# A tanh of a zero ahead of ScalarE's loads, and a first weight load in two pieces, in a decode attention and MLP kernel

## The chip, the cores and the metric

The kernel runs on one core of one Trainium2 chip. The metric is the device time of one execution in microseconds; the figure for a kernel is the median of its runs. Beside the times there is a profile of one execution, with its own time and its span (from its first to its last recorded instruction).

## What is computed

One decode step for two sequences (B = 2, one token each, D = 1024). A gate mixes an attention block with a cache (32 heads, 16384 cached positions, head size 128) and an MLP block. In short:

```python
def reference(A_x, A_k_cache, A_v_cache, A_wq, A_wo, B_x, B_w1, B_w2, B_w3, B_w4, gate_w):
    x = A_x                                                   # [2, 1, 1024], bf16
    g = sigmoid((x * gate_w).sum(-1, keepdims=True))
    q = (x @ A_wq) split into 32 heads
    a = softmax(q . k_cache * 128 ** -0.5) . v_cache, heads joined, @ A_wo
    hs = shift(gelu(layernorm(x) @ w1)) @ w2      # S is 1: the shift leaves only zeros
    x1 = x + hs
    b = x1 + gelu(layernorm(x1) @ w3) @ w4
    return g * a + (1 - g) * b
```

The caches are 2 x 268 MB in bf16, wq and wo 8.4 MB each, w2 2.1 MB, w3 and w4 7.3 MB each. All of it is read once.

## The kernel before, in words

**A plan written out by hand.** `_Plan` (line 24) holds a list of operations for each engine. `pl.add` (line 44) appends a compute operation and `pl.dma` (line 53) a transfer, each with the events that it waits for; `emit` (line 78) writes the lists out, so that the order of the calls in `build_kernel` is the order on each engine. A DMA raises its semaphore by 16, and the event is the sum up to then: an event on a semaphore that two DMAs raise one after the other waits for both.

**The ring.** All large data passes through one SBUF tile, `ring` (line 167): 5 slots, each 128 partitions x 16384 bf16, which is 32 KB a partition. `queue_load` puts a load into a list, `pump` (line 300) issues from it on SP as long as the slots of the next load are free, and `release` (line 311) frees slots at the event of the last reader. A slot has a semaphore (`s_ring`, line 225); loads in several pieces took those of `s_tail` (line 230), which before were only the pieces of the second half of wo. The order of the list is fixed: the two halves of wq into slots 0 and 1, w2 into slot 2, the halves of w3 into 3 and 4, those of w4 into 0 and 1 (line 335), then for each of 32 pairs of heads a K load and a V load (8.4 MB and two slots each), and at the end wo. SP issues nothing else but half of the output, so its queue is the stream of all weights and caches. A weight load is made by `runs` (line 321): partition p gets a run of neighbouring rows of the matrix, for a half of wq 4 rows of 4096 bf16, 32 KB in one piece, of a matrix in which the partitions lie 64 KB apart.

**The start.** GpSimd builds constants with a chain of memsets and selects (`pconst`, lines 238 to 275), the last being `xrow` at line 275. VectorE reduces some of them (lines 277 to 282; the reduction at line 277 waits for `ev_rowm`, that at line 279 for the whole chain). ScalarE's list begins with DMAs: x, two rows of 2 KB (line 560), the gate's weights, one row of 2 KB (line 561), and four pieces of x for the last sum (line 563), which wait for GpSimd's `xrow`. PE transposes x and the gate's weights (line 583) when both are there, VectorE copies the result into `xT_bf` and `xT_f` (lines 587 and 588), and PE multiplies the halves of wq with it (line 604: 256 matmuls; the last of a half releases the half's slot). The gate (`st_gate`, line 392) is a tanh on ScalarE (line 399), its first activation. The MLP's matmuls follow (lines 466, 495 and 537), with another tanh at line 448.

**The loop.** For a pair of heads VectorE transposes K in place in 8 pieces (`do_T`, line 647), PE makes the scores (`do_S`, line 653), the softmax goes through VectorE, PE and ScalarE (lines 663 to 680, with the exponential at line 674), PE multiplies with V (`do_PV`, line 689), and the result is scaled (`do_out`, lines 698 to 703). K's two slots are released one by one at line 653, V's at line 689. The end (`do_aproj`, lines 707 to 726) multiplies with wo and adds the MLP's part; line 750 copies the sum out.

Of the kernel before, what the change touches and what calls it, by code (L numbers as in the profile page):

```python
# [6 lines left out]
ACT = mybir.ActivationFunctionType  # L7
# [3 lines left out]
F32 = mybir.dt.float32  # L11
# [109 lines left out]
def build_kernel(nc, A_x, A_k, A_v, A_wq, A_wo, B_w1, B_w2, B_w3, B_w4, gate_w, out, dbg=None):  # L121
# [4 lines left out]
    HD = H * Dh  # L126
    assert Sq == 1 and Dh == 128 and D % 128 == 0 and F % 128 == 0 and B == 2
    P = 128
# [17 lines left out]
    scale = float(Dh) ** -0.5  # L146
    eps = 1e-5
    NEG_BIG = -30000.0
    RQ = NBD // 2
# [6 lines left out]
    assert QO * RO == Dh and RO == 2 * RS  # L156
    wo_runs = [[(0, RS)], [(RS, RS // 2), (RS + RS // 2, RS // 4), (RO - RS // 4, RS // 8), (RO - RS // 8, 1), (RO - 1, 1)]]
    assert all(sum(n for _, n in runs) == RS for runs in wo_runs)
    NQ = 4
    DQ = D // NQ  # L160
# [3 lines left out]
    with ExitStack() as st:  # L164
        block = st.enter_context(nc.Block())
        sb = lambda name, shape, dt: st.enter_context(nc.sbuf_tensor(name, shape, dt))
        ring = sb("ring", [P, NRS, SLOT], BF16)
# [51 lines left out]
        gin = sb("gin", [P, 2], F32)  # L219
        gT = sb("gT", [P, 4], F32)  # L220
        th = sb("th", [P, 2], F32)
        banks = [st.enter_context(nc.psum_tensor(f"ps{i}", [P, 512], F32)) for i in range(8)]
        sem = lambda n: st.enter_context(nc.semaphore(n))
        esems = {e: sem("e_" + e) for e in ENGS}
        s_ring = [sem(f"dr{i}") for i in range(NRS)]
# [4 lines left out]
        s_tail = [sem(f"dtl{i}") for i in range(len(wo_runs[1]))]  # L230
        pl = _Plan(esems)
# [6 lines left out]
        def pconst(fn, waits=()):  # L238
            pprev[0] = pl.add("pool", fn, waits=tuple(waits) + (pprev[0],), sig=True)
            return pprev[0]  # L240
# [29 lines left out]
        for hp in range(HP):  # L270
# [3 lines left out]
        pconst(aff(m24[:, :, :], 0, [[-1, 2], [-32, NQ]], 1), (e0,))  # L274
        ev_xr0 = pconst(lambda e: e.memset(xrow[:, :], 0.0))
        ev_const = pprev[0]
        e0 = pl.add("dve", lambda e: e.tensor_reduce(rowv[:, :], rowm[:, :, :].rearrange("p a b -> p (a b)"), axis=AX.X, op=ALU.add),
                    waits=(ev_rowm,), sig=True)
        ev_m2 = pl.add("dve", lambda e: e.tensor_reduce(m2[:, :], m24[:, :, :], axis=AX.X, op=ALU.add), waits=(ev_const,), sig=True)
# [3 lines left out]
                        waits=(e0,), sig=True)  # L283
# [16 lines left out]
        def pump():  # L300
            while dma_q and all(i in slot_free for i in dma_q[0][2]):
                key, fns, slots = dma_q.pop(0)
                waits = sum((slot_free.pop(i) for i in slots), ())
                slot_of[key] = slots[0]
                slots_of[key] = slots
                for k, fn in enumerate(fns):
                    dsem = s_ring[slots[0]] if len(fns) == 1 else s_tail[k]
                    dma_done[key] = dma_done[key, k] = pl.dma("sp", (lambda e, fn=fn, idx=slots[0]: fn(e, idx)), dsem,
                                                              waits=waits if k == 0 else ())

        def release(key, ev, slots=None):
            for idx in slots or slots_of[key]:
                assert idx not in slot_free
                slot_free[idx] = tuple(ev) if isinstance(ev, (tuple, list)) else (ev,)
            pump()
# [2 lines left out]
            assert key in dma_done, f"load {key} not yet issued in program order (would deadlock)"  # L318
            return dma_done[key]

        def runs(Wt, width, r0, rn, base=0):
            def fn(e, idx):
                src = Wt.rearrange("(p r) n -> p (r n)", p=P)[:, r0 * width:(r0 + rn) * width]
                return e.dma_start(ring[:, idx, (r0 - base) * width:(r0 - base + rn) * width], src)  # L324
            return fn

        wloads = {}
        for hi in range(2):
            wloads[("wq", hi)] = [runs(A_wq, HD, hi * RQ, RQ, hi * RQ)]
            wloads[("w3", hi)] = [runs(B_w3, F, hi * RQ, RQ, hi * RQ)]  # L330
            wloads[("w4", hi)] = [runs(B_w4, D, hi * RF, RF, hi * RF)]
            wloads[("wo", hi)] = [runs(A_wo, D, r0, rn, hi * RS) for r0, rn in wo_runs[hi]]
# [211 lines left out]
        key = ("w2", 0)  # L544
        put([row_stage(key, list(range(NBD)), 0, NBD, lambda kc: shT_bf[:, kc, :], "const", last=True), hs_columns], key)
        put([st_x1, ln_a(x1T_f[:, :, :], "x1", st2_ps, "xn2"), ln_b(st2_ps, "xn2", None)])
        for hi in range(2):
            key = ("w3", hi)
# [3 lines left out]
        for hi in range(2):  # L552
            key = ("w4", hi)
# [3 lines left out]
        put([st_bg])  # L557

        ev_bg0 = pl.add("dve", lambda e: e.memset(bgrow[:, :], 0.0), sig=True)
        ev_x = pl.dma("act", lambda e: e.dma_start(xg_row[0:2, :], A_x[:, 0, :]), s_misc)  # L560
        ev_gw = pl.dma("act", lambda e: e.dma_start(xg_row[2:3, :], gate_w.rearrange("(o d) -> o d", o=1)), s_gw)
        for qd in range(NQ):
            ev_xr = pl.dma("act", lambda e, qd=qd: e.dma_start(xrow[32 * qd:32 * qd + 2, :], A_x[:, 0, qd * DQ:(qd + 1) * DQ]), s_xr,
                           waits=(ev_xr0,))
# [8 lines left out]
        for pi in range(2):  # L573
            queue_load(("wo", pi), wloads[("wo", pi)], ((4, 3)[pi],))
        pump()

        def xcols(row, b_n, nb):
# [4 lines left out]
        for nb in range(NBD):  # L582
            last = pl.add("pe", lambda e, nb=nb: e.transpose(tr_ps[:, nb * 4:nb * 4 + 3], xcols(xg_row, 3, nb), ident[0:3, 0:3]),
                          waits=(ev_x, ev_gw, ev_ident), sig=(nb == NBD - 1))
# [10 lines left out]
        for hi in range(2):  # L595
            key = ("wq", hi)
            ev_arr = arrived(key)
            wv = ring_w(slot_of[key], RQ, HD)
            for r in range(RQ):
                kc = hi * RQ + r  # L600
                for h in range(H):
                    lastmm = (h == H - 1)
                    def fn(e, h=h, r=r, kc=kc, wv=wv, first=first):
                        return e.matmul(q_ps[:, h, :], lhsT=wv[:, r, h * Dh:(h + 1) * Dh], rhs=xT_bf[:, kc, :],  # L604
                                        start=first, stop=(kc == NBD - 1), skip_group_check=True)
# [6 lines left out]
        for bp in range(NBP):  # L612
            evp = pl.add("pe", lambda e, bp=bp: e.matmul(q4_ps[:, bp, :], lhsT=PermQ[:, bp, :],
                                                        rhs=q_sb[:, :, :].rearrange("p h b -> p (h b)"), start=True, stop=True),
                         waits=(ev_q, ev_const, ev_r0), sig=(bp == NBP - 1))
# [135 lines left out]
        for b, eng in enumerate(("sp", "act")):  # L751
            ev_out = pl.dma(eng, lambda e, b=b: e.dma_start(out[b, 0, :].rearrange("(q n) -> q n", q=NQ), orow[b:PR:32, :]), s_out[b],
                            waits=(ev_fin,))
# [28 lines left out]
def bass_gated_mix__mha_block_cached__mixer_s_mlp__decode_kernel(  # L782
    nc: bass.Bass,
    A_x: bass.AP,
    A_k_cache: bass.AP,
    A_v_cache: bass.AP,
    A_wq: bass.AP,
    A_wo: bass.AP,
    B_x: bass.AP,
    B_w1: bass.AP,  # L790
    B_w2: bass.AP,
    B_w3: bass.AP,
    B_w4: bass.AP,
    gate_w: bass.AP,
    out: bass.AP,
):
    build_kernel(nc, A_x, A_k_cache, A_v_cache, A_wq, A_wo, B_w1, B_w2, B_w3, B_w4, gate_w, out)
# [28 lines left out]
```

## Time and profile before

| what | value |
| --- | --- |
| median of 3 runs | 1326.1 us (1325.9 to 1326.19) |
| the profiled execution | 1325.93 us |
| its span | 1324.1 us |
| busy: PE, VectorE, ScalarE, GpSimd | 785.1, 657.2, 45.7, 23.5 us |
| DMA traffic | 570.60 MB, 431 GB/s over the span |

In the profile DVE is VectorE, ACT is ScalarE, POOL is GpSimd, PEld the weight loads of PE. SPq and ACTq are the issues of DMAs on SP and ACT, which count as no busy time. A row of a timeline gives the start and the time from the first to the last of its instructions in us, engine, line, operation, output <- input, their count, and in brackets how long the engine had been idle before and what ended it. A row of the windows gives the stretch, its length, busy time and count for each engine (PE, PEld, DVE, ACT, POOL), the granted clock of PE, the share in which the 16 DMA engines were busy, and GB/s. A row of the waits gives the engine and line, what it waited for, us in total, times, and the longest. A row of one line's instructions gives their durations in ns (min/median/max) and their first and last start.

### The profile page before, as it was taken

The numbers are of one execution on the slowest core, as the hardware profiler recorded it, in microseconds if no ns is written. First come the engines' busy times: TensorE is split into PE (matmuls) and PEld (weight loads), VectorE is DVE, ScalarE is ACT, GpSimd is POOL, SyncE is SP. The second block draws the span as 40 slices with busy tenths as digits, with TensorE's granted clock in tenths as the row PEclk, the third lists the DMA queues.
The fourth block names the chain that finished last, engine by engine and source line by source line (L and its number), as shares of the span: only waits on it lengthen the run. The fifth ranks groups of instructions, "written<-read, shape, count | busy, mean of one in ns | idle before, by whom it ended". The sixth has DMA issues, their size and how long they took to land.

```text
span 1324.1 us, 12290 instructions
## 1 busy us (share of the span) xinstructions
PE 785.1 (59%) x5235; PEld 335.8 (25%) x5235; DVE 657.2 (50%) x523; ACT 45.7 (3%) x99; POOL 23.5 (2%) x110
## 2 busy tenths in 40 slices
PE   3645557656556765555676555566655456665646
PEld 2512223222222322222232222222222222222223
DVE  1054446655444665544466554446655444665543
ACT  0000000000000000000000000000000000000000
POOL 3000000000000000000000000000000000000000
PEclk9966787777678777767877776788787788878679
DMA  9999999999999999999999999999999999999998
GB/s 403 445 424 434 436 434 434 432 438 432 430 440 432 430 440 430 430 440 430 434 436 430 438 434 436 432 432 438 434 428 440 432 430 440 430 432 438 430 434 359
DMA packets 11138, 570.60 MB, mean 431 GB/s; under 512 B 1252, under 2 KB 1268, under 8 KB 1655
## 3 DMA queue, kind: packets, MB, share of 16 engines
q1 hardware_dynamic: 11096, 570.43, 99.7%
q8 instruction: 8, 0.13, 0.0%
q10 hardware_dynamic: 30, 0.01, 0.0%
q14 instruction: 4, 0.02, 0.0%
HBM read 570.44 MB, written 0.00 MB: 431 GB/s over the span
## 4 chain that ended last, share of the span: by engine, by line
DMA 70%; PE 23%; DVE 6%; issue 0%; SPq 0%
DMA ring<-in_A_k_cache_dram 65%; PE ps L653 23%; DVE ring L647 6%; DMA ring<-in_B_w_dram 3%; DMA ring<-in_A_wo_dram 2%; PE ps L466 1%; SPq L324 0%; DVE orow L750 0%; PE ps L726 0%
## 5 line engine op out<-in xcount | busy, mean ns | idle before, releaser
L653 PE MATMUL ps<-ring,Z 128*128 128x512 bf16 x2048 | 534.5, 420 | 389.1 <-DVE ring L647 388.5
L647 DVE STREAM_TRANSPOSE ring<-ring 128x2048 f32<-128x2048 f32 x256 | 565.2, 2275 | 278.6 <-DMA ring<-in_A_k_cache_dram 278.6
L653 PEld LDWEIGHTS ps<-ring,Z 128*128 128x128 bf16 x2048 | 204.4, 104 | 706.7 <-issue 473.5
L689 PE MATMUL ps<-ring,PT_sb 128*32 128x512 bf16 x2048 | 168.2, 501 | 4.1 <-DVE recip L680 3.7
L703 DVE SCALAR_TENSOR_TENSOR OT_sb<-ps,gT,recip 128x2 f32 x32 | 7.0, 220 | 203.4 <-PE ps L700 203.4
L689 PEld LDWEIGHTS ps<-ring,PT_sb 128*32 128x32 bf16 x2048 | 67.6, 122 | 90.8 <-issue 69.6
L674 ACT ACTIVATE P_sb<-ps,negm 128x512 bf16<-128x512 f32 x32 | 22.0, 687 | 1013.9 <-DVE negm L672 1013.9
L663 DVE TENSOR_REDUCE rA<-ps 128x1 f32<-128x512 f32 x32 | 22.1, 692 | 64.1 <-PE ps L653 64.1
L678 PE MATMUL ps<-rowsum,hsel 128*128 128x1 f32 x128 | 24.0, 291 | 37.9 <-ACT P_sb L674 37.9
L676 DVE STREAM_TRANSPOSE PT_sb<-P_sb 128x512 bf16<-128x512 bf16 x32 | 22.8, 711 | 27.0 <-ACT P_sb L674 27.0
L634 POOL TENSOR_TENSOR Z<-q_f,mask 128x8 bf16<-128x8 f32 x64 | 12.3, 227 | 1214.3 <-PE ps L653 1214.3
L678 PEld LDWEIGHTS ps<-rowsum,hsel 128*128 128x128 f32 x128 | 21.3, 236 | 40.7 <-ACT P_sb L674 40.7
L665 PE MATMUL ps<-ident,rmax_bf 128*1 128x128 bf16 x32 | 6.9, 217 | 33.1 <-DVE rmax_bf L664 33.1
L698 ACT ACTIVATE acc_sb<-ps 128x512 bf16<-128x512 f32 x32 | 19.1, 597 | 198.8 <-PE ps L689 198.8
L700 PE MATMUL ps<-dsel,acc_sb 128*128 128x2 bf16 x128 | 8.1, 167 | 22.5 <-ACT acc_sb L698 22.5
L466 PE MATMUL ps<-xn_bf,ring 128*128 128x2 bf16 x224 | 14.5, 202 | 2.9 <-DMA ring<-in_B_w_dram 2.9
L466 PEld LDWEIGHTS ps<-xn_bf,ring 128*128 128x128 bf16 x224 | 14.4, 172 | 3.0 <-DMA ring<-in_B_w_dram 3.0
L700 PEld LDWEIGHTS ps<-dsel,acc_sb 128*128 128x128 bf16 x128 | 5.3, 96 | 38.2 <-ACT acc_sb L698 38.2
L665 PEld LDWEIGHTS ps<-ident,rmax_bf 128*1 128x1 bf16 x32 | 2.5, 79 | 48.9 <-DVE rmax_bf L664 48.9
L604 PE MATMUL ps<-xT_bf,ring 128*128 128x2 bf16 x256 | 7.1, 165 | 11.7 <-DVE xT_f L588 7.4
L666 DVE TENSOR_REDUCE m_sb<-ps 1x2 bf16<-1x128 bf16 x32 | 8.9, 278 | 9.9 <-PE ps L665 9.9
L672 DVE TENSOR_SCALAR negm<-ps,cAB 128x1 f32<-128x1 f32 x32 | 8.9, 277 | 9.2 <-PE ps L669 9.2
(97 smaller groups left out, 85.8 us busy)
## 6 DMA issues: line engine op xcount, KB each, us to landing
ring<-in_B_w_dram SPq DMA_DIRECT2D x4, 3584.0 KB, 35.4
ring<-in_A_wq_dram SPq DMA_DIRECT2D x2, 4096.0 KB, 17.5
ring<-in_A_wo_dram SPq DMA_DIRECT2D x1, 4096.0 KB, 40.2
ring<-in_B_w_dram SPq DMA_DIRECT2D x1, 2048.0 KB, 27.1
ring<-in_A_wo_dram SPq DMA_DIRECT2D x1, 2048.0 KB, 22.2
ring<-in_A_wo_dram SPq DMA_DIRECT2D x1, 1024.0 KB, 24.4
ring<-in_A_k_cache_dram SPq DMA_DIRECT2D x32, 26.8
ring<-in_A_v_cache_dram SPq DMA_DIRECT2D x32, 29.2
```

The costliest lines, as they stand in the source:

```text
L466: fn = lambda e, nb=nb, kl=kl: e.matmul(out_ps[:, nb, :], lhsT=cols(wv, kl, nb, nout), rhs=rhs_of(k0 + kl), start=False, stop=True, skip_g ...
L634: ev = pl.add("pool", lambda e, hp=hp: e.tensor_tensor(Z[:, :, ZO:ZO + P].rearrange("p t (i c) -> p t i c", c=32)[:, :, 2 * hp:2 * hp + 2, ...
L647: return pl.add("dve", lambda e: e.transpose(ap, ap), waits=(arrived(("k", n)),), sig=True)
L653: ev = pl.add("pe", lambda e, bp=bp: e.matmul(S_ps[:, 0:NCOL], lhsT=Z[:, bp, ZO - 2 * u:ZO - 2 * u + P], rhs=kv[:, :, bp // 2, :, bp % 2], ...
L663: e1 = pl.add("dve", lambda e: e.tensor_reduce(rA[:, :], S_ps[:, 0:NCOL], axis=AX.X, op=ALU.max), waits=(ev_S[n],), sig=True)
L665: e3 = pl.add("pe", lambda e: e.transpose(mt_ps, rmax_bf[:, :], ident[:, :]), waits=(e2,), sig=True)
L674: e7 = pl.add("act", lambda e: e.activation(P_sb[:, :], S_ps[:, 0:NCOL], ACT.Exp, bias=negm[:, 0:1], scale=scale, accum_out=rowsum[:, 0:1] ...
L676: e8 = pl.add("dve", lambda e: e.transpose(PT_sb[:, :], P_sb[:, :]), waits=(e7,), sig=True)
L678: e9 = pl.add("pe", lambda e, hp=hp: e.matmul(l_ps[:, hp:hp + 1], lhsT=hsel[:, hp, :], rhs=rowsum[:, 0:1], start=True, stop=True, skip_gro ...
L689: ev = pl.add("pe", lambda e, jj=jj, cg=cg: e.matmul(acc_ps[32 * cg:32 * cg + 32, 0:512], lhsT=PT_sb[:, 32 * jj:32 * jj + 32], rhs=vv[:, 4 ...
L698: e1 = pl.add("act", lambda e: e.activation(acc_sb[:, :], acc_ps[:, 0:512], ACT.Copy), waits=(ev_pv,), sig=True)
L700: e2 = pl.add("pe", lambda e, w=w: e.matmul(oT_ps, lhsT=acc_sb[:, w * P:(w + 1) * P], rhs=dsel[:, w, :], start=(w == 0), stop=(w == 3)), w ...
```

## The change

ScalarE's list gets a first operation ahead of its DMAs: a tanh of one column of `th0`, a new tile of 128 x 2, into its other column; VectorE's list gets a memset of `th0` to zero as its first operation, on which the tanh waits. The two halves of wq were one DMA each; the first is now two, of partitions 0 to 15 and of partitions 16 to 127, one after the other on SP and with the same columns. Both raise the slot's semaphore, so that the readers wait for both. Nothing else moves: in the order of the built program ScalarE has the table load and the new tanh ahead of the loads of x, and no table load at the gate's tanh; SP has 16 x 16384, 112 x 16384 and 128 x 16384 elements of wq where there were two of 128 x 16384; VectorE has the memset first; PE and GpSimd are as before.

```diff
+        th0 = sb("th0", [P, 2], F32)
...
+        ev_t0 = pl.add("dve", lambda e: e.memset(th0[:, :], 0.0), sig=True)
         e0 = pl.add("dve", lambda e: e.tensor_reduce(rowv[:, :], rowm[:, :, :].rearrange("p a b -> p (a b)"), axis=AX.X, op=ALU.add),
...
-                    dsem = s_ring[slots[0]] if len(fns) == 1 else s_tail[k]
+                    dsem = s_tail[k] if key[0] == "wo" and len(fns) > 1 else s_ring[slots[0]]
...
-        def runs(Wt, width, r0, rn, base=0):
+        def runs(Wt, width, r0, rn, base=0, ps=slice(0, P)):
             def fn(e, idx):
-                src = Wt.rearrange("(p r) n -> p (r n)", p=P)[:, r0 * width:(r0 + rn) * width]
-                return e.dma_start(ring[:, idx, (r0 - base) * width:(r0 - base + rn) * width], src)
+                src = Wt.rearrange("(p r) n -> p (r n)", p=P)[ps, r0 * width:(r0 + rn) * width]
+                return e.dma_start(ring[ps, idx, (r0 - base) * width:(r0 - base + rn) * width], src)
             return fn
...
-            wloads[("wq", hi)] = [runs(A_wq, HD, hi * RQ, RQ, hi * RQ)]
+            wloads[("wq", hi)] = [runs(A_wq, HD, hi * RQ, RQ, hi * RQ, ps) for ps in ((slice(0, 16), slice(16, P)) if hi == 0 else (slice(0, P),))]
...
+        pl.add("act", lambda e: e.activation(th0[:, 1:2], th0[:, 0:1], ACT.Tanh, scale=0.5), waits=(ev_t0,))
         ev_x = pl.dma("act", lambda e: e.dma_start(xg_row[0:2, :], A_x[:, 0, :]), s_misc)
```

## The prediction

> **What bounds the kernel now.** I read the page first: the 40 slices and the queue table, then the chain that ended last.
>
> ```profile
> span 1324.1 us, 12290 instructions
> DMA  9999999999999999999999999999999999999998
> GB/s 403 445 424 434 436 434 434 432 438 432 430 440 432 430 440 430 430 440 430 434 436 430 438 434 436 432 432 438 434 428 440 432 430 440 430 432 438 430 434 359
> q1 hardware_dynamic: 11096, 570.43, 99.7%
> DMA 70%; PE 23%; DVE 6%; issue 0%; SPq 0%
> ```
>
> One queue, SP's, moves 570.43 MB and keeps the 16 DMA engines occupied for 99.7% of the span. Only the first slice (403) and the last (359) lie clearly under the 430 to 440 GB/s of the rest. The chain also names PE (23%) and DVE (6%), so I looked at one turn of the loop in the chain in order of time, and at the line that issues K.
>
> ```profile
> 94.89 26.17 DMA ring<-in_A_k_cache_dram
> 121.08 2.32 DVE ring L647
> 123.52 9.49 PE ps L653 x32
> 133.02 26.75 DMA ring<-in_A_k_cache_dram
> ...
> L349 SPq DMA_DIRECT2D ring<-in_A_k_cache_dram x32: 327/328/328, 53.3 to 1255.7; - x32
> DMA to landing us min/median/max: 26.2/26.8/29.0
> ```
>
> A K load is 128 rows of 64 KB, 8.39 MB: alone it would take 19.3 us at 434 GB/s. It lands 26.2 us or more after its issue, so some 6.9 us of the previous V load are still ahead of it: whenever PE frees a slot and SP issues, the engines have work left. PE and DVE in the chain are where the issue was made, not a time in which the DMA engines ran dry. The windows say the same.
>
> ```profile
> 5.00:60.00 55.00, 29.77 (x594) 26.59 (x594) 7.64 (x35) 1.70 (x3) 8.26 (x31) 1.00 1.00 429
> 130.00:1280.00 1150.00, 692.39 (x4152) 282.45 (x4150) 597.15 (x446) 41.24 (x90) 11.52 (x60) 0.78 1.00 434
> ```
>
> The last two columns are DMA share and GB/s: 1.00 and 434 over 1150 us, 1.00 and 429 in the prologue. **So the time is the moment at which bytes begin to flow, plus 570 MB at 434 GB/s, plus the tail. A microsecond gained or lost in the first loads arrives at the end whole**, as nothing later has room to absorb it. The change touches only the first microseconds, so I read these on the timelines of SP, ACT, DVE and PE, and in narrow windows.
>
> ```profile
> 0.74 0.87 SPq L324 DMA_DIRECT2D ring<-in_A_wq_dram  x2
> 1.65 26.30 SPq L324 DMA_DIRECT2D ring<-in_B_w_dram  x5
> 0.74 0.55 ACTq L560 DMA_DIRECT2D xg_row<-in_A_x_dram  x1
> 1.33 0.24 ACTq L561 DMA_DIRECT2D xg_row<-in_gate_w_dram  x1
> 16.41 1.28 ACT L399 ACT_TABLE_LOAD   x1 [16.41 <-issue]
> 29.93 0.17 ACT L399 ACTIVATE th<-ps 128x2 f32<-128x2 f32 x1 [12.24 <-PE ps L389]
> 8.11 0.63 PE L583 MATMUL ps<-ident,xg_row 3*128 3x3 bf16 x8 [8.11 <-DMA xg_row<-in_gate_w_dram]
> 16.15 3.55 PE L604 MATMUL ps<-xT_bf,ring 128*128 128x2 bf16 x128 [7.41 <-DVE xT_f L588]
> 13.66 0.22 DVE L277 TENSOR_REDUCE rowv<-rowm 128x1 f32<-128x64 f32 x1 [13.66 <-POOL rowm L243]
> 15.23 0.16 DVE L279 TENSOR_REDUCE m<-m 128x2 f32<-128x8 f32 x1 [1.35 <-POOL xrow L275]
> 15.90 0.10 DVE L587 COPY xT_bf<-ps 128x16 bf16<-128x16 bf16 x1
> 0.50:1.00 0.50, 0.00 (x0) 0.00 (x0) 0.00 (x0) 0.00 (x0) 0.20 (x1) 1.00 0.00 0
> 1.50:1.75 0.25, 0.00 (x0) 0.00 (x0) 0.00 (x0) 0.00 (x0) 0.20 (x1) 1.00 0.27 8
> 1.75:2.00 0.25, 0.00 (x0) 0.00 (x0) 0.00 (x0) 0.00 (x0) 0.20 (x1) 1.00 5.07 1450
> ```
>
> SP begins its first issue at 0.74 us; the first bulk packets are counted at about 1.75 us, 1.0 us later (a packet is counted whole in the window where it starts, hence 1450). The first weight tile is not needed at once: PE's first matmuls on it (L604) wait for xT until 16.15 us, and xT waits on VectorE behind two reductions that wait for GpSimd's constants.
>
> **The change, part by part.**
>
> *The tanh on ScalarE.* It adds one VectorE memset of 128x2 (about the 0.10 us of L587), on an engine that is idle until 13.66 us, and one activation of 0.17 us (as L399's). The table load of 1.28 us is no new work: it moves from 16.41 us to the start. There it stands ahead of ScalarE's loads of x and of the gate, which are issued 1.28 + 0.17 = 1.45 us later, at about 2.2 and 2.8 us. The four loads behind them (xrow) wait for GpSimd until 15.2 us anyway and do not move. Who waits for x: PE's transposes at 8.11 us, then about 9.6; done at 10.2 us; and VectorE asks for them at 15.90 us. Cover 5.6 us, so I cost it at nothing. Were the cover gone, L604 would begin later and give its slot back later, behind which the sixth load stands:
>
> ```profile
> SPq L324 <- PE ps L604: 24.0, 2, 16.5
> 46.04 7.26 PE L466 MATMUL ps<-xn_bf,ring 128*128 128x2 bf16 x112 [1.25 <-DMA ring<-in_B_w_dram]
> ```
>
> The loads issued before that one run until 46 us, while the slot is free at 19.7 us: another 26 us of cover. The old place of the table load, 16.41 to 17.69 us, lay in ScalarE's idle time ahead of the tanh at 29.93 us: taking it away gains nothing. Gone from the first microsecond is ACT's issue beside SP's.
>
> *The split.* One more issue on SP, 0.24 us (the one-row load of L561) to 0.41 us:
>
> ```profile
> L324 SPq DMA_DIRECT2D ring<-in_A_wq_dram x2: 392/402/412, 0.7 to 1.2; - x2
> ...
> DMA to landing us min/median/max: 12.2/25.4/43.2
> ```
>
> The later loads are issued that much later, but each has over 10 us of bytes queued ahead of it: nothing. The first issue, now of 16 rows instead of 128, may be shorter: at best as short as the one row (0.24 for 0.39), 0.15 us earlier first bytes; at worst no gain. The first bytes could at most come the whole 1.0 us earlier that lies between issue and data. I take 0.1 us.
>
> Against that stands the shape. 16 rows of 32 KB are 0.524 MB, 1.21 us of stream at 434 GB/s **if they move at full rate**. No row of this trace shows that: every large load here, of 16, 28, 32 or 64 KB a row, lies over all 128 partitions, and all run at the one flat 434 GB/s. The flat ceiling may be the engines' (then any 16 partitions over 16 engines are as fast) or the destination's (then it shrinks with the partitions reached). Bounds: with the engines' ceiling the loss is 0. With the destination's, at its strictest, each partition takes 434/128 = 3.39 GB/s: the first piece takes 0.524 MB / 54 GB/s = 9.66 us instead of 1.21, a loss of 8.45 us; the second, 112 partitions at 380 GB/s, 9.66 us instead of 8.45, a loss of 1.21. Together 9.66 us. In between lies a destination that is shared by groups of partitions, with 16 engines crowding on few groups. I take the middle, 4.8 us: the loads that show the ceiling show it independent of row length, which speaks for a place that all rows of one kind share, and 16 neighbouring rows are the worst case for that.
>
> [...]
>
> *Sum.* Profiled execution: 1325.93 us, of which 1324.1 are the span and 1.8 lie around it; it is 0.17 us under the median of 1326.1. Loss 4.8, gain 0.1, the rest 0: 1325.93 + 4.7 = 1330.6 us, and on the median **1330.8 us**.
>
> **The rivals.**
>
> *A: the ceiling is the engines'.* The 16 rows go one to each engine at full rate; what stays is the earlier start, 0 to 1.0 us, likeliest 0.1 to 0.4: 1325.8 us, not slower. For it: 434 GB/s over 16 engines is 27.1 GB/s each whatever the rows' length, and a 32 KB row an engine is the same piece of work as before. It decides if the destination of a row plays no part. Chance 0.36.
>
> *B: the strict destination.* Both pieces run at the rate of their partitions, or the engines that fall behind in the second piece stay behind, as each later load lands with its slowest engine: 9.5 us, 1335.6 us. For it: 1.00 share leaves no later pause in which a late engine could catch up. Against it: the second piece still covers 7/8 of the partitions. Chance 0.13.
>
> *C: x comes too late or nothing is new.* If x landed over 7 us later, PE's start would move, but the 26 us of cover keep it from the stream: 1326.1 us. The same if the two pieces are merged into an unchanged stream. Chance 0.03.
>
> *D: more than 2.7 us gained.* Between the span's start and the first bytes lie only 1.75 us; I see no such gain. Chance 0.02.
>
> **How the numbers follow.** Forecast, with a loss between 2.7 and 7.5 us (1328.8 to 1333.6): 0.46. Within 0.2% (2.65 us, about what a measurement of this kernel can tell from no change) end A and C: 0.39. Slower: forecast and B, 0.59. Faster: D, 0.02. As both a small gain and a loss hold much of the chance, the range reaches from A with a gain of 0.7 us, 1325.4, to the strict bound, 1335.7; the forecast's own range is 1328.8 to 1333.6.
>
> **What would show it.** In the changed profile: SP issues three loads of A_wq; the windows between 2 and 7 us should move well under 434 GB/s (right) or the same as now (A). The first weight tile, now landed 12.2 us after its issue at 0.74, so at 12.9 us, should land near 17.7 and PE's L604 start then instead of at 16.15; the first K load, now issued at 53.33 us, near 58. The loop must keep its 434 GB/s (38.7 us for the 16.8 MB of a turn): if the loss arises there, my reason is wrong. The table load at about 0.7 us and the transposes near 9.6 us, with L587 still at 15.9, would show the first part free. I am wrong if the first 0.5 MB flow at the full rate, or if a late start is made up later.

## The result, and the profile after

The changed kernel takes 1335.62 us (median of 6 runs, 1335.23 to 1335.8) against 1326.05 us (6 runs, 1325.89 to 1326.19): **9.6 us slower**, a ratio of 1.0072 with a 95% interval of 1.0059 to 1.0085. Its profiled execution took 1335.59 us, with a span of 1333.7 us; 1.9 us lie around the span (1.8 before).

From the page of the changed kernel, the lines that answer to those of the prediction:

```profile
span 1333.7 us, 12293 instructions
DMA  9999999999999999999999999999999999999998
GB/s 282 432 443 435 425 440 427 436 436 430 434 432 436 428 438 428 436 436 428 440 427 436 434 432 430 436 436 428 438 428 436 434 430 440 427 436 430 436 430 357
q1 hardware_dynamic: 11112, 570.43, 99.7%
```

The bytes are the same, 570.43 MB, and the engines are again busy for 99.7% of the span. Only the first slice differs clearly: 282 GB/s where it was 403. A slice is 33.3 us, so 121 GB/s less are about 4.0 MB not moved there, which take 9.3 us at 434 GB/s. The whole loss lies in the first slice. Narrower windows, first of the kernel before, then of the changed one (the last two columns are the share of time in which the DMA engines were busy, and GB/s):

```profile
1.50:7.00 5.50, 0.00 (x0) 0.00 (x0) 0.00 (x0) 0.00 (x0) 4.23 (x15) 1.00 1.01 382
7.00:22.00 15.00, 4.18 (x136) 4.07 (x136) 2.00 (x10) 1.28 (x1) 5.60 (x25) 1.00 1.00 429
22.00:32.00 10.00, 6.37 (x166) 5.15 (x166) 1.86 (x10) 0.17 (x1) 0.00 (x0) 1.00 1.02 432
```

```profile
1.50:7.00 5.50, 0.00 (x0) 0.00 (x0) 0.00 (x0) 0.72 (x2) 4.23 (x15) 1.00 1.22 191
7.00:22.00 15.00, 0.63 (x8) 0.57 (x8) 2.00 (x10) 0.00 (x0) 5.60 (x25) 1.00 0.94 245
22.00:32.00 10.00, 3.57 (x128) 3.49 (x128) 0.00 (x0) 0.00 (x0) 0.00 (x0) 1.00 0.97 413
130.00:1280.00 1150.00, 702.16 (x4146) 283.63 (x4150) 605.64 (x449) 40.65 (x89) 11.51 (x60) 0.78 1.00 434
```

**A busy share near 1 with half the rate: the engines have packets in hand all the time, but the packets take longer.** The trace holds every packet with its duration: of the first 128 packets of the queue, 32 KB each, the median took 1.21 us before and 2.17 us in the changed kernel. After 22 us the rate comes back to 413 GB/s, and in the loop it is the 434 GB/s of before. The issues of the changed kernel with their time to landing (last column, us) say which loads these were; the whole first half of wq landed 12.2 us after its issue before:

```profile
ring<-in_A_wq_dram SPq DMA_DIRECT2D x1, 512.0 KB, 7.3
...
ring<-in_A_wq_dram SPq DMA_DIRECT2D x1, 3584.0 KB, 21.5
```

An eighth of the bytes takes 7.3 us to land; the rest lands 21.5 us after its own issue, at 22.7 us. The timelines of the changed kernel's SP, ScalarE, PE and VectorE, and its first K load and transpose in the chain:

```profile
0.74 1.34 SPq L326 DMA_DIRECT2D ring<-in_A_wq_dram  x3
0.73 1.28 ACT L562 ACT_TABLE_LOAD   x1 [0.73 <-PEq L814]
0.91 0.55 ACTq L563 DMA_DIRECT2D xg_row<-in_A_x_dram  x1
2.03 0.20 ACT L562 ACTIVATE th<-th 128x1 f32<-128x1 f32 x1
11.74 0.63 PE L586 MATMUL ps<-ident,xg_row 3*128 3x3 bf16 x8 [11.74 <-POOL dsel L244]
15.90 0.10 DVE L590 COPY xT_bf<-ps 128x16 bf16<-128x16 bf16 x1
22.77 3.57 PE L607 MATMUL ps<-xT_bf,ring 128*128 128x2 bf16 x128 [10.40 <-DMA ring<-in_A_wq_dram]
```

```profile
62.50 29.05 DMA ring<-in_A_k_cache_dram
91.55 0.02 issue
91.57 2.32 DVE ring L650
```

PE now waits for the weights (22.77 us), no longer for xT. The first K load is issued at 62.50 instead of 53.33 us, 9.2 us later, and its first transpose starts at 91.57 instead of 82.38, 9.2 us later too. At the end the span is 9.6 us longer. The transposes of x start at 11.74 us, 3.6 us later than before; the copy that waits for them starts at 15.90 as before, so this delay is covered.

### The profile page after: what moved, and what is told of

It is laid out like the page before. It is cut to its first block, busy times and chain, and to the rows that moved or that the text cites. A ratio compares the mean times of both kernels' runs of the same rounds, so it can differ in the third digit from the quotient of the medians.

```text
span 1333.7 us, 12293 instructions
## 1 busy us (share of the span) xinstructions
PE 790.2 (59%) x5235; PEld 335.3 (25%) x5235; DVE 657.0 (49%) x524; ACT 45.9 (3%) x100; POOL 23.5 (2%) x110
## 3 DMA queue, kind: packets, MB, share of 16 engines
q1 hardware_dynamic: 11112, 570.43, 99.7%
## 4 chain that ended last, share of the span: by engine, by line
DMA 70%; PE 23%; DVE 6%; issue 0%; SPq 0%; another core or an unknown queue 0%
DMA ring<-in_A_k_cache_dram 65%; PE ps L656 22%; DVE ring L650 6%; DMA ring<-in_B_w_dram 3%; DMA ring<-in_A_wo_dram 2%; PE ps L468 1%; SPq L326 0%; DVE orow L753 0%; PE ps L729 0%
## 5 line engine op out<-in xcount | busy, mean ns | idle before, releaser
L656 PEld LDWEIGHTS ps<-ring,Z 128*128 128x128 bf16 x2048 | 200.7, 103 | 702.2 <-issue 453.8
L692 PE MATMUL ps<-ring,PT_sb 128*32 128x512 bf16 x2048 | 177.2, 522 | 4.6 <-DVE recip L683 4.6
## 6 DMA issues: line engine op xcount, KB each, us to landing
ring<-in_A_wq_dram SPq DMA_DIRECT2D x1, 3584.0 KB, 21.5
```

The lines of the kernel that those rows point to most:

```text
L656: ev = pl.add("pe", lambda e, bp=bp: e.matmul(S_ps[:, 0:NCOL], lhsT=Z[:, bp, ZO - 2 * u:ZO - 2 * u + P], rhs=kv[:, :, bp // 2, :, bp % 2], ...
L692: ev = pl.add("pe", lambda e, jj=jj, cg=cg: e.matmul(acc_ps[32 * cg:32 * cg + 32, 0:512], lhsT=PT_sb[:, 32 * jj:32 * jj + 32], rhs=vv[:, 4 ...
```

## The experiments

**Theories.** My theory: the loss is the shape of the two pieces; destination partitions share a rate in groups, so that a load into few of them is slow. Why they should was my supposition, that several DMA engines crowd on one way in; no view of the profile shows such a way. Rivals: a strict rate for each partition (the prediction's strict bound, which gives 9.66 us, almost exactly the measured 9.6), the source (16 engines reading neighbouring rows of HBM), the tanh, or the mere fact of one more, small load.

### Each half of the change alone

```diff
 e1_tanh_only, against the kernel before (with the tile th0 and its memset):
...
+        pl.add("act", lambda e: e.activation(th0[:, 1:2], th0[:, 0:1], ACT.Tanh, scale=0.5), waits=(ev_t0,))
         ev_x = pl.dma("act", lambda e: e.dma_start(xg_row[0:2, :], A_x[:, 0, :]), s_misc)
 e2_split_only, against the changed kernel (the tile th0 and its memset go too):
...
-        pl.add("act", lambda e: e.activation(th0[:, 1:2], th0[:, 0:1], ACT.Tanh, scale=0.5), waits=(ev_t0,))
```

> Only the tanh of the zero and its memset, the first weight load whole. My theory (the loss is the two pieces' shape): 1326.0 to 1326.1, no change, with the transposes about where they are before (8.1 us). Rival (the earlier table load or the later x costs part of the 9.6 us): several us more, up to 1335.

> Only the split into 16 and 112 partitions, no tanh. My theory: the whole loss, 1335.6, and the first piece lands about 7.3 us after its issue as in the changed kernel. Rival (the tanh takes part): less than 1335.

Measured: the tanh alone 1325.99 us against 1325.98 (ratio 1.0, 0.9991 to 1.001), the split alone 1335.76 us (1.0073, 1.0057 to 1.009). The split is the whole loss, the tanh costs nothing that can be seen. The first piece of the split alone lands after 6.9 us, a little less than the expected 7.3. From the timelines of PE and ScalarE with the tanh alone:

```profile
7.92 0.63 PE L586 MATMUL ps<-ident,xg_row 3*128 3x3 bf16 x8 [7.92 <-DMA xg_row<-in_gate_w_dram]
16.14 3.56 PE L607 MATMUL ps<-xT_bf,ring 128*128 128x2 bf16 x128 [7.60 <-DVE xT_f L591]
0.73 1.28 ACT L562 ACT_TABLE_LOAD   x1 [0.73 <-PEq L814]
0.91 0.56 ACTq L563 DMA_DIRECT2D xg_row<-in_A_x_dram  x1
```

ScalarE issues its first DMA at 0.91 us, while the table load runs until 2.01 us; with the tanh alone the transposes start even a little earlier than before (7.92 for 8.11 us). With the split alone they do so too:

```profile
7.22 0.63 PE L583 MATMUL ps<-ident,xg_row 3*128 3x3 bf16 x8 [7.22 <-DMA xg_row<-in_gate_w_dram]
```

So the 11.74 us of the changed kernel need both halves. The view puts that wait down to GpSimd's `dsel`, of which the transposes read nothing; they wait for the two loads and for `ident`, which was done by 1.5 us, so it must have been one of the loads. In the trace the last of their three rows moves at 8.4 us, where it was 6.4 before. What held it is not shown.

### The same bytes cut the other way

```diff
+        def cut(c0, cn):
+            def fn(e, idx):
+                src = A_wq.rearrange("(p r) n -> p (r n)", p=P)[:, c0:c0 + cn]
+                return e.dma_start(ring[:, idx, c0:c0 + cn], src)
+            return fn
...
-            wloads[("wq", hi)] = [runs(A_wq, HD, hi * RQ, RQ, hi * RQ)]
+            wloads[("wq", hi)] = [cut(c0, cn) for c0, cn in ((0, HD // 2), (HD // 2, RQ * HD - HD // 2))] if hi == 0 else [runs(A_wq, HD, RQ, RQ, RQ)]
```

> The first load in two pieces of the same bytes, 0.5 and 3.5 MB, but cut by columns (4 KB and 28 KB a row), each over all 128 partitions, no tanh. My theory (few partitions are slow): 1326.1, no loss, at best 0.3 us gained. Rival (one load more, or a first load that small, costs by itself): slower by 2 to 10 us.

Measured: 1326.46 us against 1325.98 (1.0004, 0.9994 to 1.0013): 0.5 us more in the medians, inside the interval, and nowhere near 9.6. One load more, or a small first load, is not the cause. It brought no gain either.

### Split at 32 partitions: groups or single partitions

Against the changed kernel, without its tanh:

```diff
-            ... ((slice(0, 16), slice(16, P)) if hi == 0 else (slice(0, P),))]
+            ... ((slice(0, 32), slice(32, P)) if hi == 0 else (slice(0, P),))]
```

> The split at 32 partitions instead of 16, no tanh. [...] Strict theory (every partition has its own 3.4 GB/s): the first piece takes 9.7 us, lands 12 us after its issue, and the total is 1335.7.

Measured: 1335.69 us (1.0073, 1.0056 to 1.009). The total is that of the strict theory, but a rate shared by groups would give as much if the second piece is slow too. The landing separates them. The first piece, in the issues of this kernel:

```profile
ring<-in_A_wq_dram SPq DMA_DIRECT2D x1, 1024.0 KB, 7.5
```

Twice the bytes of the 16 partitions land after 7.5 us, the same time, not after 12. A whole load of 4.19 MB lands after 12.2 us, of which 9.66 are its bytes at 434 GB/s; the other 2.5 us I take, as an estimate, for all that is not bytes. Less these, 1.05 MB took 5.0 us, 210 GB/s, and in the changed kernel 0.524 MB took 4.8 us, 109 GB/s (119 by the 6.9 us of the split alone): about a half and a quarter of the full rate. One rate for each partition would give 108 and 54. **The strict theory falls, and with it the reason that I gave for rival B, though its time came out.**

The other piece, of 96 partitions, was slow as well. In the trace the first 128 packets, which are those of the two pieces, took 1.85 to 2.77 us, 2.41 on average, where the median before was 1.21. Eight for each of 16 engines make 19.3 us, 9.6 us more than the bytes at 434 GB/s, and that is the whole loss.

### A load in front, to separate source, destination and shape

Six kernels (one is the price of the bytes) have the first weight load whole and one more load ahead of it, into slot 4, whose own load waits for it; nobody reads what it brings. The 1330.8 us of the expectations are what the 1325.98 us before and the 4.8 us that 0.524 MB took in the changed kernel add up to. If the destination is at fault, the same bytes spread over more partitions (x16s8, x128c) must take less; if the source is, the source rows set apart (x16src8). DST and SRC stand for the two sides of the load, which are listed at the end of the diff.

```diff
...
+                if key == ("w3", 1):
+                    waits = waits + (ev_extra,)
...
+            ev_extra = pl.dma("sp", lambda e: e.dma_start(DST, SRC), s_ex)
         for n in range(NPR):
             q_k(n)
...
 # W = A_wq.rearrange("(p r) n -> p (r n)", p=P)
 x16      DST = ring[0:16, 4, :]          SRC = W[0:16, 0:SLOT]
 x16s8    DST = ring[0:P:8, 4, :]         SRC = W[0:16, 0:SLOT]
 x16src8  DST = ring[0:16, 4, :]          SRC = W[0:P:8, 0:SLOT]
 x128c    DST = ring[:, 4, 0:SLOT // 8]   SRC = W[:, 0:SLOT // 8]
 x112     DST = ring[16:P, 4, :]          SRC = W[16:P, 0:SLOT]
 x128     DST = ring[:, 4, :]             SRC = W[:, 0:SLOT]
```

> The kernel before with one more load in front: 16 rows of 32 KB of wq (source rows 0 to 15) into partitions 0 to 15 of slot 4, whose own load waits for it; nobody reads them. The first weight load is whole. 0.52 MB more are 1.2 us at the full rate. [...] Rival (a late start or a boundary of loads, not the rate): 1327.2.

> The same extra bytes from the same source rows 0 to 15, but into partitions 0, 8, 16, ... 120. [...] Theory of the source: as the load into partitions 0 to 15, 1330.8.

> The same destination partitions 0 to 15 but the source rows 0, 8, 16, ... 120, eight times as far apart. Theory of the destination: as with neighbouring rows, 1330.8. Theory of the source: nearer to the full rate, 1327.2 to 1328.4.

> The same number of bytes in one extra load over all 128 partitions, 4 KB a row. Theory of the destination: 1.2 us and what a load with short rows costs at the start (0.5 us in the cut by columns), so 1327.3 to 1327.8. Rival (any small load in front is slow): 1329 and more.

> The kernel before with an extra load in front of partitions 16 to 127 (3.67 MB, into slot 4, read by nobody). At the full rate 8.45 us. Theory: 112 rows over 16 engines make 7 neighbouring rows each, engines meet on the same ways in, and the 6.5 us of the loss that the first piece alone does not explain (9.6 less 3.1) belong to this shape by itself: 8.45 + 6.5, so 1341.0. Rival: the second piece is only slow because the first left the engines out of step; by itself it loses no more than the 1.2 us of its missing eighth: 1335.7.

> The same with all 128 partitions (4.19 MB): 9.66 us of stream at 434 GB/s and no loss, 1335.7; it gives the price of the bytes. Were an extra load in front costly by itself, more.

The "more" column is against the kernel before on the same chip (1326.07 us for the first four, 1326.0 for the last two), "bytes" what the extra bytes take at 434 GB/s, "over" the difference of the two:

| kernel | us | ratio (95%) | more | bytes | over |
| --- | --- | --- | --- | --- | --- |
| x16 | 1330.33 | 1.0033 (1.002 to 1.0045) | 4.26 | 1.21 | 3.05 |
| x16src8 | 1330.59 | 1.0034 (1.0021 to 1.0046) | 4.52 | 1.21 | 3.31 |
| x16s8 | 1328.65 | 1.002 (1.001 to 1.0029) | 2.58 | 1.21 | 1.37 |
| x128c | 1327.68 | 1.0012 (1.0002 to 1.0022) | 1.61 | 1.21 | 0.40 |
| x112 | 1340.59 | 1.0108 (1.0092 to 1.0125) | 14.59 | 8.45 | 6.14 |
| x128 | 1335.65 | 1.0072 (1.0056 to 1.0089) | 9.65 | 9.66 | 0 |

The landings of the extra load, one fence for each kernel, in the order x16, x16src8, x16s8, x128c, x112, x128:

```profile
ring<-in_A_wq_dram SPq DMA_DIRECT2D x1, 512.0 KB, 6.9
```

```profile
ring<-in_A_wq_dram SPq DMA_DIRECT2D x1, 512.0 KB, 7.3
```

```profile
ring<-in_A_wq_dram SPq DMA_DIRECT2D x1, 512.0 KB, 5.1
```

```profile
ring<-in_A_wq_dram SPq DMA_DIRECT2D x1, 512.0 KB, 3.9
```

```profile
ring<-in_A_wq_dram SPq DMA_DIRECT2D x1, 3584.0 KB, 17.0
```

```profile
ring<-in_A_wq_dram SPq DMA_DIRECT2D x1, 4096.0 KB, 12.2
```

**For the 16 partitions it is the destination.** The source rows eight times as far apart change little (4.52 for 4.26, intervals that overlap); with the same source rows, the destination partitions spread from 0 to 120 take 2.58 us instead of 4.26 (landing 5.1 instead of 6.9); and 128 partitions take the same bytes in 1.61. Sixteen partitions spread by eight behave like the 32 neighbours, about half the full rate (5.1 less 2.5 is 2.6 us for 0.524 MB, 202 GB/s, where the 32 had 210). Which partitions share a rate, and through what, no run shows.

**112 partitions are slower than 128 in absolute time**: 14.6 us for 3.67 MB, 9.65 us for 4.19 MB. The windows of x112 show the busy share and the rate while the piece is under way, and x128's the same stretch:

```profile
5.00:15.00 10.00, 0.62 (x8) 0.56 (x8) 0.22 (x1) 0.00 (x0) 6.98 (x28) 1.00 1.00 262
```

```profile
5.00:15.00 10.00, 0.63 (x8) 0.57 (x8) 0.22 (x1) 0.00 (x0) 7.00 (x28) 1.00 1.01 436
```

262 GB/s for 436 at the same busy share (1.00 and 1.01). So the second piece is slow by itself, without a first one that leaves the engines out of step: the rival of that experiment, 1335.7, falls. The 16 partitions that it leaves out are not reason enough either: they are an eighth, and the rate is 40% lower.

The packets of the trace exclude two more reasons. The first 112 packets of x112 took 1.39 to 2.62 us, 2.01 on average (262 GB/s over 16 busy engines make 2.0 us a packet of 32 KB too); the first 128 of x128 took 1.21 us at the median. None of the 112 was as short as that, so it is not one late engine that held up the rest. And the busy share is a mean over 16 engines: at 1.00 none stood idle, so it is not that fewer engines took part. The packets follow one another, end to start, in 16 chains with seven of the 112 in each; seven at 2.01 us make 14.1 us, near the measured 14.59.

**Why the packets of 112 partitions take longer is not shown.** The missing eighth of the partitions accounts for at most 1.21 us of the 6.14, by one rate for each partition. That engines meet at the destination remains my supposition, as it is for the 16 partitions. Which rows each engine takes was not observed, so the seven neighbouring rows of the expectation are not shown either. Nor did a run read the 112 rows from elsewhere in wq: the source is excluded for the 16 partitions alone.

**The sum closes**: 3.05 us over for the 16 partitions and 6.14 for the 112 make 9.19 us, which is how much later the first K load is transposed in the changed kernel (91.57 for 82.38). The rest of the 9.6 us arises behind the last K load: this lands at 1291.32 us for 1282.10, still 9.2 later, and the last piece of wo at 1330.51 for 1321.05, 9.5 later. Why is not shown.

## Why the prediction was right in sign and wrong in size

- **What bounds the kernel: right.** The time is the start of the stream plus its bytes; the loss of the first 22 us reached the end whole, at an unchanged 434 GB/s in the loop, and the 9.65 us of x128 are its bytes to within 0.01.
- **The tanh at nothing: right, but not by the steps that I gave.** I had the loads of x 1.45 us later, behind the table load. They are issued at 0.91 instead of 0.74 us: ScalarE's DMAs did not wait for it. The transposes, which I had near 9.6 us, start at 11.74 all the same, and in neither half of the change alone. The cover that I counted, up to the copy at 15.90, was needed, and it sufficed.
- **0.1 us gained by a shorter first issue: wrong, too small to matter.** In the chain of the changed kernel the first issue, of 16 rows, takes 0.41 us, no less than the 0.39 of 128:

```profile
0.74 0.41 SPq L326
```

- **The two pieces at 4.8 us: the step that failed, in size.** I bounded the first piece between 0 and 8.45 us; it cost about 3.05, below the middle of 4.2. I bounded the second at 1.21 us, by the partitions that it leaves out, with a middle of 0.6; it cost about 6.14, five times that bound. The bound was no bound: it took for granted that a piece loses only by the partitions that it leaves out. Two errors of opposite sign left the sum at half of the measured 9.6.
- **The signs.** The windows between 2 and 7 us did move well under 434 GB/s (191 from 1.5 to 7 us). But the first weight tile was complete for PE at 22.77 us instead of near 17.7, and the first K load was issued at 62.50 us instead of near 58: both late by the second piece.
- **The rivals.** A (the ceiling is the engines') is refuted by x16s8 against x16: the same rows and bytes, other partitions, another time (1328.65 us for 1330.33). B had the time (1335.6) by two mechanisms. A rate for each partition is refuted by the 32 partitions; engines that fall behind and stay behind are not what x112 shows, where all packets were slow (1.39 us and more, where the median of x128 was 1.21). C and D are out. The measured 1335.62 us lies outside the forecast's own range (1328.8 to 1333.6) and just inside the whole range, which reached to 1335.7 only because of the strict bound: that part was luck.

## What to carry to other kernels

A load that streams at the full rate over 128 partitions need not keep that rate in parts of them. None of the cuts by partitions measured here kept it (16 and 112 lost 9.6 us, 32 and 96 lost 9.7), while a cut by columns cost 0.5 us at most in the medians. Where a first load has to come in pieces, try columns first, and do not take 112 partitions for 7/8 of 128 (14.59 us for 9.65 here). Where the DMA share is full, compare the GB/s of the same stretch too: the share counts engines that hold packets, not bytes that move (262 and 436 GB/s at a share near 1, in x112 and x128). In this kernel, bound by one stream, a delay of that stream in its first 22 us was paid at the end whole (9.2 us late at the first K load, 9.6 us at the end); a delay beside it, the 3.6 us of the transposes, cost nothing that can be seen.

## What was not expected of the hardware

- 3.67 MB into partitions 16 to 127 added 14.6 us, 4.19 MB into all 128 added 9.65.
- ScalarE issued a DMA at 0.91 us in the middle of its table load (0.73 to 2.01 us) and ahead of an activation that stands before it in its list (2.03 us).
- A small first load with rows of 4 KB cost 0.4 to 0.5 us over its bytes in the medians (x128c and the cut by columns), where a whole one with rows of 32 KB cost none (x128). In both cases the 95% interval also allows no cost at all.
